# State products beside the next unit's score products, and key transposes one step later

## The chip, the cores and the metric

The kernel runs on one core of one Trainium2 chip. The metric is the device time of one execution in microseconds (us). TensorE is PE, VectorE DVE, ScalarE ACT, GpSimd POOL; SP is the engine whose queue issues the DMAs.

## The reference

A gated linear attention over 4 batches, 8 heads, 768 time steps and a head dimension of 48, then two feed-forward layers over 3072 tokens (384 to 2048 to 384 features):

```python
f = 1.0 / (1.0 + np.exp(-f_logit))
for t in range(S):
    state = f[:, :, t, :, None] * state + np.einsum('bhd,bhe->bhde', k[:, :, t], v[:, :, t])
    y[:, :, t] = np.einsum('bhd,bhde->bhe', q[:, :, t], state)
...
r = np.maximum(x @ w_in, 0.0)
x = (r * r) @ w_out                      # first layer
h = x @ w_in2
x = (h * np.tanh(log1p(exp(h)))) @ w_out2  # second layer
```

## The kernel before

The attention is cut into 24 units: 12 chunks of 64 time steps, each in two halves that hold two batches (y = 0 and 1) and 8 heads. A unit is worked in these pieces, each a small function: the decay (v_min, a_exp, a_ln, v_scan, a_dq, a_dk), q and k times the decay (v_q, v_k), the scores k'q (m_a, PE, tile aq), their causal mask (v_mask), the transposes of k (m_t, PE, tile tr) and their copy to SBUF (a_kn), the output (m_y, PE, tile y) and its copy (a_y), six DMAs that rearrange it (y_dma, ay to ax), its split for the first layer (a_x, v_x), and the product k v that renews the state (m_u, PE, tile uq) with the addition and decay of the state (v_s). The inputs of unit i+2 are loaded by load_f and load_v.

The first layer runs through 96 steps (six blocks of 512 tokens times 16 slices of the hidden dimension). Step j issues do_l1(j), nine matmuls of 128x128 by 128x512 into a PSUM tile h (line 332), and do_l2(j-2), nine more into three accumulators (line 343). Each product is three matmuls, since both factors are split into a high and a low part. Between them ACT and DVE make the activation: act_a(j-1) is a Relu that reads h (line 714), a square and a rounded copy gh; act_b(j-1) is the remainder gl on DVE (line 356). Beside this the weights of the second layer are unpacked (w2_load, w2_abs, w2_bits, w2_split), three steps a slice.

The order is written out by hand. The table START holds the beginning, up to unit 8 and step 18. After it, `put(step, prio, f, ...)` enters a function in a step, and `run` calls a step's functions by rising prio; each engine then works its own instructions in that order. Unit i has s = 4i - 17: m_a in step s behind l1, m_y in step s+2, so that unit i's step s+4 is unit i+1's step s. QUAD = 9: from unit 9 on, aq and uq are computed in four quadrants of 64 by 64, and each takes two PSUM tiles (y = 0, 1).

h, aq, tr, y and uq all come from one PSUM pool with one tag and five buffers; a tile is free when its readers are done:

```python
h_p = ctx.enter_context(tc.tile_pool(name="hps", bufs=5, space=PSUM))
...
a = [h_p.tile([128, 4, C], F32, tag="h", name="aq") for _ in range(2)]
...
u = [h_p.tile([128, 4, D], F32, tag="h", name="uq") for _ in range(2)]
```

Of the kernel before, what the change touches and what calls it, by code (L numbers as in the profile page):

```python
# [22 lines left out]
QUAD = 9  # L23
# [189 lines left out]
def fast_path(ctx: ExitStack, tc: tile.TileContext, flag, qkf, vv, w1, w2, out):  # L213
# [22 lines left out]
    late, done = [], set()  # L236
# [143 lines left out]
    def attention(at, at1):  # L380
# [268 lines left out]
        def put(s, prio, f, *a):  # L649
            todo.setdefault(s, []).append((prio, len(todo.get(s, [])), f, a))  # L650
# [6 lines left out]
        def unit(i, s):  # L657
            put(s - 4, 24, v_min, i)
            put(s - 3, 15, a_exp, i)
            put(s - 3, 31, a_ln, i)  # L660
            put(s - 2, 25, v_scan, i)
            put(s - 2, 32, a_dq, i)
            put(s - 2, 32, a_dk, i)
            put(s - 1, 26, v_q, i, 0)
            put(s - 1, 26, v_q, i, 1)
            put(s - 1, 26, v_k, i)
            put(s - 1, 26, v_end, i)
            put(s + 4 if i >= 8 else 19 + i, 33, v_fmin, i)
            put(s, 110, m_a, i)
            put(s, 111, m_t, i)  # L670
            put(s + 1, 10, v_mask, i, 0)
            put(s + 1, 10, v_mask, i, 1)
            put(s + 1, 14, a_kn, i)
            put(s + 2, 110, m_y, i)
            put(s + 2, 111, m_u, i)
            put(s + 3, 12, a_y, i)
            if i < NE:
                put(s + 3, 112, m_x, i)
            else:
                put(s + 3, 12, y_dma, i)  # L680
            put(s + 3, 22, v_s, i, 0)
            put(s + 3, 22, v_s, i, 1)
            put(s + 4, 16, a_x, i)
            put(s + 4, 30, v_x, i)
            if i < NU - 2:
                put(s + 1, 50, load_f, i + 2)
                put(s + 1, 50, load_v, i + 2)

        for i in range(NU):
            unit(i, (-16, -14, -12, -10, 3, 5, 8, 11)[i] if i < 8 else 4 * i - 17)  # L690
# [252 lines left out]
```

## Time and profile before

| | |
|---|---|
| median of 3 runs | 902.0 us (901.57 to 902.25) |
| profiled execution | 902.64 us, span 900.9 us |
| PE busy | 882.6 us (98%) |
| DVE busy | 676.5 us (75%) |
| ACT busy | 619.0 us (69%) |
| line 332, h (l1 of both layers) | 1728 matmuls, 426.5 us |
| line 343, a (l2 of both layers) | 1146 + 573 matmuls, 388.3 + 223.6 us |

Units 9 to 23 lie between 137 and 430 us of the span, in the second and third of six blocks and what adjoins them. Busy time of PE is modelled, so the chain of waits, which says at each moment what the end waited for, is the better guide; the timelines show each engine's own order, with the idle time before an instruction and what ended it in square brackets.

### The profile page before, as it was taken

What the parts mean: (1) busy time and instruction counts of PE and PEld (TensorE: products, weight loads), DVE (VectorE), ACT (ScalarE), POOL (GpSimd) and SP (SyncE); (2) the same over time, 40 slices, a digit from 0 to 9 for tenths busy, and PEclk for the clock granted to TensorE, in tenths of its full rate; (3) what the DMA queues carried; (4) which work ended last, traced back from release to release, by engine and by line L of the source; (5) the groups of instructions that cost most, each with busy time, mean ns of one, the idle gap of its engine ahead of it and who ended that gap; (6) DMA issues with size and microseconds to landing.
All of it is one profiled execution on the core that took longest, in us unless ns stands there. A gap on an engine that the chain in (4) does not pass through costs nothing.

```text
span 900.9 us, 15172 instructions
## 1 busy us (share of the span) xinstructions
PE 882.6 (98%) x5849; PEld 724.0 (80%) x5849; DVE 676.5 (75%) x1146; ACT 619.0 (69%) x1131; POOL 5.4 (1%) x21
## 2 busy tenths in 40 slices
PE   6899999999999999999999999999999999999997
PEld 6788888888788888778888888888888888888885
DVE  7999976776877878772221788788888788888785
ACT  7798776885887678674544666676666676666664
POOL 2000000000000000000000000000000000000000
PEclk7899999999999999999999999999999999999999
DMA  9972233465536455532453200200200100200001
GB/s 240 349 174 105 68 98 82 156 197 158 189 123 223 135 191 180 186 125 77 169 190 139 71 1 0 71 1 1 71 0 1 71 1 1 71 1 1 36 0 39
DMA packets 34287, 89.93 MB, mean 100 GB/s; under 512 B 5216, under 2 KB 11360, under 8 KB 34208
## 3 DMA queue, kind: packets, MB, share of 16 engines
q1 hardware_dynamic: 34208, 88.89, 30.9%
q8 instruction: 48, 0.79, 0.4%
q14 instruction: 31, 0.25, 0.1%
HBM read 63.70 MB, written 22.02 MB: 95 GB/s over the span
## 4 chain that ended last, share of the span: by engine, by line
PE 96%; DVE 1%; ACT 1%; DMA 1%; issue 1%; SPq 0%; ACTq 0%; DVEq 0%
PE h L332 44%; PE a L343 43%; PE y L524 2%; PE tr L485 1%; PE aq L470 1%; PE at L475 1%; PE y L517 1%; DMA in<-in_qkf_dram 1%; PE u L542 1%; PE uq L537 1%; PE xt L576 0%; ACT kn L507 0%; DVE mv L448 0%; PE a L839 0%; SPq L406 0%
## 5 line engine op out<-in xcount | busy, mean ns | idle before, releaser
L332 PE MATMUL h<-x,w 128*128 128x512 f32 x1728 | 426.5, 391 | 1.2 <-ACT x L601 0.6
L343 PE MATMUL a<-gh,w 128*128 128x512 f32 x1146 | 388.3, 393 | 0.0
L332 PEld LDWEIGHTS h<-x,w 128*128 128x128 f32 x1728 | 324.8, 188 | 70.6 <-DVE x L605 0.9
L343 PEld LDWEIGHTS a<-gh,w 128*128 128x128 f32 x1146 | 215.2, 188 | 46.1
L343 PE MATMUL a<-gl,w 128*128 128x512 f32 x573 | 223.6, 391 | 0.0
L781 ACT ACTIVATE e<-e 128x512 f32<-128x512 f32 x95 | 60.1, 632 | 117.5 <-DVE e L780 117.5
L356 DVE TENSOR_TENSOR gl<-r,gh 128x512 fp32r<-128x512 f32 x96 | 65.8, 686 | 80.3 <-ACT gh L351 79.9
L343 PEld LDWEIGHTS a<-gl,w 128*128 128x128 f32 x573 | 107.7, 188 | 21.7 <-DVE gl L356 0.4
L780 DVE TENSOR_SCALAR e<-h 128x512 f32<-128x512 f32 x95 | 65.7, 692 | 60.8 <-PE h L332 58.2
L714 ACT ACTIVATE r<-h 128x512 f32<-128x512 f32 x96 | 56.7, 591 | 55.0 <-PE h L332 54.5
L775 ACT ACTIVATE r<-u,cst 128x512 f32<-128x512 f32 x94 | 67.9, 723 | 8.7 <-DVE u L789 2.7
L789 DVE SCALAR_TENSOR_TENSOR u<-e 128x512 f32<-128x512 f32 x95 | 65.9, 694 | 10.1 <-ACT e L781 0.7
L356 DVE TENSOR_TENSOR gl<-g,gh 128x512 fp32r<-128x512 f32 x95 | 65.7, 691 | 0.0
L777 DVE TENSOR_TENSOR e<-h,u 128x512 f32<-128x512 f32 x94 | 64.2, 683 | 0.0
L784 DVE TENSOR_TENSOR g<-e,r 128x512 f32<-128x512 f32 x94 | 64.2, 682 | 0.0
L351 ACT ACTIVATE gh<-r 128x512 fp32r<-128x512 f32 x96 | 60.7, 633 | 3.1
L715 ACT ACTIVATE r<-r 128x512 f32<-128x512 f32 x96 | 60.7, 632 | 3.1
L351 ACT ACTIVATE gh<-g 128x512 fp32r<-128x512 f32 x95 | 60.2, 633 | 3.0 <-DVE g L808 0.8
L776 ACT ACTIVATE r<-r 128x512 f32<-128x512 f32 x94 | 59.5, 633 | 3.0
L507 ACT ACTIVATE kn<-tr 64x192 f32<-64x192 f32 x88 | 28.4, 322 | 7.5 <-PE tr L485 6.6
L605 DVE TENSOR_TENSOR x<-ax,x 128x384 fp32r<-128x384 f32 x16 | 8.9, 556 | 32.5 <-ACT x L601 32.5
L433 DVE TENSOR_TENSOR_SCAN es<-es,cap 112x520 f32<-112x520 f32 x24 | 29.6, 1235 | 3.1 <-ACT es L429 3.0
(120 smaller groups left out, 707.2 us busy)
## 6 DMA issues: line engine op xcount, KB each, us to landing
r<-in_w_dram SPq DMA_DIRECT2D x16, 768.0 KB, 11.9
sr<-in_w_dram SPq DMA_DIRECT2D x32, 384.0 KB, 3.7
w2d<-sw SPq DMA_DIRECT2D x32, 384.0 KB, 3.4
w<-w2d SPq DMA_DIRECT2D x32, 384.0 KB, 3.5
in<-in_qkf_dram SPq DMA_DIRECT2D x18, 672.0 KB, 5.7
vs<-in_vv_dram SPq DMA_DIRECT2D x48, 96.0 KB, 5.5
x2d<-ot SPq DMA_DIRECT2D x18, 256.0 KB, 2.1
x<-x2d SPq DMA_DIRECT2D x6, 768.0 KB, 5.2
```

The costliest lines, as they stand in the source:

```text
L332: T.matmul(out=ps, lhsT=w[:, k * 128:(k + 1) * 128], rhs=x[:, s, k], start=(i == 0), stop=(i == 8))
L343: T.matmul(out=acc[m], lhsT=w[:, m * 128:(m + 1) * 128], rhs=gx, start=(fc == 0 and i == 0), stop=(fc == FC - 1 and i == 2))
L351: A.activation(out=gh, in_=g, func=AF.Copy)
L356: V.tensor_tensor(out=gl, in0=g, in1=gh.bitcast(F32), op=ALU.subtract)
L715: A.activation(out=r, in_=r, func=AF.Square)
L775: A.activation(out=r, in_=u, func=AF.Ln, bias=two)
L776: A.activation(out=r, in_=r, func=AF.Exp, scale=-1.0)
L777: V.tensor_tensor(out=e, in0=hp, in1=u, op=ALU.mult)
L780: V.tensor_scalar(out=e2, in0=ps, scalar1=20.0, scalar2=None, op0=ALU.min)
L781: A.activation(out=e2, in_=e2, func=AF.Exp)
L784: V.tensor_tensor(out=g, in0=e, in1=r, op=ALU.mult)
L789: V.scalar_tensor_tensor(out=u2, in0=e2, scalar=2.0, in1=e2, op0=ALU.add, op1=ALU.mult)
```

## The change

For units from QUAD on (`late`), four entries move: the transposes m_t from step s to s+1 and their copy a_kn from s+1 to s+2; the state products m_u from s+2 to s+4 and the state's renewal v_s from s+3 to s+5; the load load_f of unit i+2 from s+1 to s+2. Since s+4 is the next unit's s, m_u(i) comes right behind m_a(i+1). Units 22 and 23 have no m_t, m_u or v_s, so it concerns those of units 9 to 21. All else is the same, line numbers from 670 on are one or more higher.

```diff
             put(s, 110, m_a, i)
-            put(s, 111, m_t, i)
+            late = i >= QUAD
+            put(s + late, 111, m_t, i)
             put(s + 1, 10, v_mask, i, 0)
             put(s + 1, 10, v_mask, i, 1)
-            put(s + 1, 14, a_kn, i)
+            put(s + 1 + late, 14, a_kn, i)
             put(s + 2, 110, m_y, i)
-            put(s + 2, 111, m_u, i)
+            put(s + 4 if late else s + 2, 111, m_u, i)
             put(s + 3, 12, a_y, i)
...
-            put(s + 3, 22, v_s, i, 0)
-            put(s + 3, 22, v_s, i, 1)
+            put(s + 5 if late else s + 3, 22, v_s, i, 0)
+            put(s + 5 if late else s + 3, 22, v_s, i, 1)
             put(s + 4, 16, a_x, i)
             put(s + 4, 30, v_x, i)
             if i < NU - 2:
-                put(s + 1, 50, load_f, i + 2)
+                put(s + 1 + late, 50, load_f, i + 2)
                 put(s + 1, 50, load_v, i + 2)
```

PE around step s of unit 10, the difference (- before, + now): h is l1, aq the scores of unit 10, tr its transposes, uq the state products of unit 9, a the accumulators of l2.

```order
 L332 MATMUL h<-x,w_777 128x512 x9
 L470 MATMUL aq<-mv_154,in_144 64x64 x16
-L485 MATMUL tr<-idn,in_144 128x112 x4
+L537 MATMUL uq<-vs_151,kn_157 48x48 x16
 L343 MATMUL a_1609<-gh,w_716 128x512
 L343 MATMUL a_1609<-gl,w_716 128x512
@@ -542,4 +541,5 @@
 L343 MATMUL a_1611<-gh,w_716 128x512
 L332 MATMUL h<-x,w_826 128x512 x9
+L485 MATMUL tr<-idn,in_144 128x112 x4
 L343 MATMUL a_1609<-gh,w_743 128x512
```

uq stands behind aq now, and tr between l1 and l2 of the next step.

DVE in steps s and s+1 of unit 11 before: x is the split of unit 10, wbit are the w2 bits, mv the masked scores, gl the remainders, sw the w2 split, es the scan.

```order
L605 TENSOR_TENSOR x<-ax,x 128x3x128
L356 TENSOR_TENSOR gl<-r,gh 128x512
L460 TENSOR_TENSOR fmin<-fmin,f 112x8
L254 TENSOR_SCALAR wbit<-wbit 128x768
L257 SCALAR_TENSOR_TENSOR wbit<-sr,wbit 128x384 x2
L260 SCALAR_TENSOR_TENSOR wbit<-sr,wbit 128x384 x2
L494 TENSOR_TENSOR mv_155<-aq,cmask 64x4x64 x4
L356 TENSOR_TENSOR gl<-r,gh 128x512
L306 SCALAR_TENSOR_TENSOR sw<-wbit,sw 128x384 x2
L433 SCALAR_TENSOR_TENSOR es_161<-es_161,cap 112x520
```

And now, from the masks on:

```order
L494 TENSOR_TENSOR mv_155<-aq,cmask 64x4x64 x4
L587 TENSOR_TENSOR vs_150<-uq,vs_152 48x4x48 x2
L588 TENSOR_TENSOR vs_150<-vs_150,f 48x384
L587 TENSOR_TENSOR vs_150<-uq,vs_152 48x4x48 x2
L588 TENSOR_TENSOR vs_150<-vs_150,f 48x384
L356 TENSOR_TENSOR gl<-r,gh 128x512
L306 SCALAR_TENSOR_TENSOR sw<-wbit,sw 128x384 x2
L433 SCALAR_TENSOR_TENSOR es_161<-es_161,cap 112x520
```

v_s of unit 10 (lines 587, 588) stands between the masks of unit 11 and gl; before, it stood ahead of the v_q of unit 11.

SP in steps 32 to 34 (unit 12), the difference: w2d are stores of the w2 split, in is load_f, vs load_v, x2d the eviction of a block, ax the first of six DMAs of y_dma.

```order
 L308 DMA w2d_0_101<-sw 128x768
 L308 DMA w2d_1_102<-sw 128x768
-L406 DMA in_144<-in_qkf_dram 112x1536
-L418 DMA vs_152<-in_vv_dram 64x384 x2
+L418 DMA vs_152<-in_vv_dram 64x384 x2
+L406 DMA in_144<-in_qkf_dram 112x1536
 L366 DMA x2d_92<-ot 128x512 x3
 L564 DMA ax<-ay 48x384
```

load_f is issued behind load_v and so nearer to the stores and to y_dma that follow.

## Rows read from the trace of the kernel before

**Rows 1.** The page, part 4: shares of the chain by engine.

```profile
PE 96%; DVE 1%; ACT 1%; DMA 1%; issue 1%; SPq 0%; ACTq 0%; DVEq 0%
```

**Rows 2.** Chain in order of time, unit 17: start us, us, what.

```profile
293.86 0.62 PE aq L470 x32
294.49 0.53 PE tr L485 x4
...
303.26 1.08 PE y L524 x32
304.34 0.51 PE uq L537 x32
304.84 2.29 PE a L343 x9
...
313.27 0.62 PE aq L470 x32
```

**Rows 3.** Chain, places where tr, aq and y stand alone.

```profile
123.27 0.39 PE tr L485 x4
123.66 2.09 PE h L332 x9
...
410.53 0.62 PE aq L470 x32
411.15 2.27 PE a L343 x9
...
419.54 1.08 PE y L524 x32
420.62 2.27 PE a L343 x9
```

**Rows 4.** Chain, the two idle stretches of PE in units 9 to 23.

```profile
234.29 1.33 issue
...
391.10 0.88 issue
```

**Rows 5.** DVE timeline ahead of the second: start us, us, line, operation, [idle before].

```profile
387.24 0.73 DVE L587 TENSOR_TENSOR vs<-uq,vs 48x192 f32<-48x192 f32 x2
...
389.89 1.39 DVE L448 TENSOR_TENSOR mv<-in,eq 48x512 f32<-48x512 f32 x2
391.20 0.68 DVE L452 TENSOR_TENSOR in<-in,es 112x512 f32<-112x512 f32 x1
```

**Rows 6.** Chain, steps 67 to 72 (units 21 and 22).

```profile
371.47 0.62 PE aq L470 x32
...
374.73 2.05 PE h L332 x9
...
391.98 0.69 PE aq L470 x32
...
394.94 2.04 PE h L332 x9
```

**Rows 7.** ACT timeline, units 14 to 21.

```profile
246.62 0.63 ACT L438 ACTIVATE eq<-es 112x512 f32<-112x512 f32 x1 [1.16 <-DVE es L433]
...
278.44 0.55 ACT L250 ACTIVATE wbit<-sr 128x384 f32<-128x384 f32 x1 [1.79 <-DMA sr<-in_w_dram]
...
314.43 0.52 ACT L601 ACTIVATE x<-ax 128x384 fp32r<-128x384 f32 x1 [3.09 <-DMA ax<-ay]
...
365.38 0.60 ACT L365 ACTIVATE ot<-a 128x512 f32<-128x512 f32 x1 [0.79 <-PE a L343]
...
375.17 0.53 ACT L601 ACTIVATE x<-ax 128x384 fp32r<-128x384 f32 x1 [4.96 <-DMA ax<-ay]
...
376.43 0.58 ACT L714 ACTIVATE r<-h 128x512 f32<-128x512 f32 x1
```

**Rows 8.** DVE timeline, unit 14: masks, remainder, split, scan.

```profile
241.99 1.78 DVE L494 TENSOR_TENSOR mv<-aq,cmask 64x256 f32<-64x256 f32 x4
243.80 0.69 DVE L356 TENSOR_TENSOR gl<-r,gh 128x512 fp32r<-128x512 f32 x1
244.41 1.02 DVE L306 SCALAR_TENSOR_TENSOR sw<-wbit,sw 128x384 fp32r<-128x384 f32 x2
245.35 1.23 DVE L433 TENSOR_TENSOR_SCAN es<-es,cap 112x520 f32<-112x520 f32 x1
```

**Rows 9.** The page, part 6: count, KB each, median us to landing.

```profile
in<-in_qkf_dram SPq DMA_DIRECT2D x18, 672.0 KB, 5.7
```

## The prediction

> **What bounds the kernel now.** I read the chain of waits first. It is TensorE (PE) for 96% of the span [rows 1], so a microsecond counts only if PE gains or loses it. In time order the chain then shows one unit of attention between the big matmuls: four steps, each of nine matmuls of l1 (line 332) and nine of l2 (line 343) at 2.04 us a group, and two small groups, aq + tr in step s and y + uq in step s+2 (s = 4i - 17 for unit i). Unit 17 takes from 293.86 to 313.27, 19.41 us [rows 2]; eight groups of 2.04 are 16.32, so the small work costs 3.09. PE idles only twice in units 9 to 23, 1.33 and 0.88 us, both ahead of aq [rows 4]. What the other engines do is read from their timelines: there the reader is to see who is late although PE does not yet wait.
>
> **The small matmuls on PE.** What the order changes is which group follows which. Behind aq the first big group takes 2.27 instead of 2.04, behind y alone also 2.27; tr takes 0.53 behind aq but 0.39 behind a big group, with 2.09 after it [rows 2, 3]. So aq, y and uq leave a tail of about 0.23, tr of 0.05, and stepping from aq to tr costs 0.14. New rows of a unit:
> - step s: aq 0.62, uq, tail 0.23. No row shows uq behind aq. Behind y it takes 0.51 [rows 2]; that is the upper end. If it saves what tr saves where nothing changes, 0.51 - 0.14 = 0.37, which I take: aq and uq are both laid out as 64x64 tiles in the built program, y as 128x64, tr and the big ones as 128x128.
> - step s+1: tr 0.39 + 0.05, some more in the next group: 0.45.
> - step s+2: y 1.08 + 0.23.
> Together 1.22 + 0.45 + 1.31 = 2.98 against 3.09: 0.11 saved in a unit, 1.4 us in the 13 units. With 0.51 for uq it is a loss of 0.03 in a unit, 0.4 us in all; with 0.32 a gain of 2.1.
> The Trainium skill, TensorEngine Tiling (Array Packing), Key Properties, says that changing the tiling mode drains the engine and changing the tile does not; by it uq behind aq has no drain, which is the value that I took. The trace has no aq followed by uq to confirm it.
>
> **The vector work that moves.** v_s(i) is two pairs of additions and two products on VectorE (DVE), 2.65 us from its start to the start of v_q behind it [rows 5]. It stood in step s+3 right ahead of v_q and v_k of the next unit, and v_k is what aq waits for: it ends at 391.88 and aq starts at 391.98 [rows 4, 5]. Moved two steps on, it no longer stands there; both idle stretches of PE go, 2.2 us. What is late next is dealt with below: v_s now stands behind the masks of the next unit, ahead of act_b and of the scan.
>
> **The new wait.** All these products go through five PSUM buffers (tag h, bufs=5). Before, step s held h, two aq and tr: four, one free. Now it holds h, two aq and two uq: all five. So l1 of step s+1 can only start when one of them has been read. In the built program it is, in 12 of the 13 places (units 10 to 22), l1's own buffer of step s: its matmuls wait for ScalarE's Relu (ACT, line 714) of the step before. (At unit 13 it is the first mask.) Before, that Relu had two steps. From l1's end to the next l1 is now 0.62 + 0.37 + 2.27, about 3.2 us. In the trace the Relu ends more than 3.1 us after l1's end in seven of the thirteen places. Take unit 21: l1 ends at 371.47, the next l1 runs from 374.73, the Relu from 376.43 for 0.58, to 377.01 [rows 6, 7]. PE would wait until 377.1, and take 0.07 to restart (aq 0.69 behind an idle stretch against 0.62 [rows 6, 3]).
> The Relu is late because ACT waits in order, first for the six transfers of y into ax (line 601 idles 3.09 and 4.96 us [rows 7]), then in some units for w2 data. Both hang on a_y, an ACT instruction half a unit earlier, so ACT, the SP queue and DVE form a loop of their own that PE hardly drives; only the slack of two steps kept it off PE.
> The Trainium skill, TensorEngine Tiling, Performance Considerations (PSUM Bottleneck), warns of just this for packed matmuls: reading PSUM out may become the bound. In the trace of before no big matmul of units 9 to 23 waits for a reader [rows 4], so by it alone nothing would be expected; the loop above is this kernel's own mechanism.
>
> **What slows that loop.** In a third of the units (14, 17, 20: those with w2_bits in step s) DVE runs without a gap from the masks over act_b and the w2 split to the scan [rows 8], and ACT's line 438 waits for this scan: 1.16 us idle at 246.62, one of three such rows of 1.13 to 1.16 [rows 7]. v_s now stands in that stretch: 2.65 later each, straight on ACT's loop. In unit 20 an eviction that waits for PE by 0.79 anyway (at 365.38 [rows 7]) takes part of it: 3 x 2.65 - 0.79 = 7.2. In the other units DVE idles there or the scan has slack. Moving a_kn one step on leaves ACT's sum up to the scan as it was: nothing.
> Against it: load_f leaves the place behind the w2 loads. In unit 16 ACT waits 1.79 for the second of them [rows 7], with the 672 KB load of in_qkf (5.7 us to landing [rows 9]) issued behind it; relief 0 to 1.8, with a smaller one in unit 19: I take 1.0. The wait of 4.96 for ax in unit 21 could fall towards 3.09 [rows 7]: 0 to 1.9, I take 0.6. X, the loop's delay at unit 21, is 7.2 - 1.0 - 0.6 = 5.6; its bounds are 0 and 9.
>
> **The sum.** At unit 21 PE waits for the loop, so what it saved earlier is swallowed and the end follows from the loop: l1 starts at 377.1 + X instead of 374.73, plus 0.07: 2.4 + X. From there to l1 of unit 22's next step it was 394.94 - 374.73 = 20.21 [rows 6]; now it is eight groups of 2.04 and 2.98: 19.30, a gain of 0.9. Behind that both kernels do the same big work. So 1.5 + X = 7.1 us. The profiled execution took 902.64 (span 900.9), which gives 909.7; the median of the runs is 902.0, 0.64 lower: **909.1 us**.
>
> **Rivals.**
> - The buffers do not bind (faster). Were the Relu to end within 3.1 us of l1 in all 13 places, PE would gain 1.4 and 2.2: 902.0 - 3.6 = 898.4. This needs ACT's wait for ax to fall from 4.96 to below about 2.5 at unit 21; units 11 and 12, where the Relu follows l1 at once, show that it can be so. Against it: moving uq out leaves PE 0.5 us earlier at the next aq while a_y comes no earlier. Chance 0.10.
> - The wait comes, but the scan does not hold ACT (X near 0): 1.5 us, 903.5. This is so if ACT is idle enough behind line 438, but it runs without a gap up to a_y there. Chance 0.12, counted as within 0.2%.
> - load_f collides with y (slower still). In the new SP order it is issued right ahead of the six transfers of y_dma. If each of nine units' ax lands 1 us later, X grows by up to 5: 914. Chance 0.08.
> - The change of neighbours saves nothing on PE. It moves 1.4 us of time that PE spends waiting anyway, and the forecast by less than 0.5.
>
> **How the numbers follow.** The forecast, slower by about 7 us, has 0.70; the collision 0.08, also slower; same 0.12; faster 0.10. A measurement of this kernel tells about 0.2% (1.8 us) from no change. The range has its low end between the second rival and the forecast's low bounds, 901.5, and its high end at the collision, 914.0; it leaves out the faster case and part of the collision.
>
> **What would show it.** In the new profile PE should have idle stretches ahead of line 332 released by ACT's Relu, in the step behind aq + uq, of 0.5 to 3 us in units 10 to 21, some 10 to 11 us in all; units 15, 16, 19 and 21 hold the most. The two stretches ahead of aq should be gone. uq behind aq should take 0.37, tr 0.39. ACT's line 438 should idle 2.6 us longer for the scan in units 14, 17 and 20. The prediction is wrong if PE stays at 98% busy without waits for ACT, if the waits stand ahead of other tiles (the masks, y), or if the small groups cost more than 3.1 a unit.

## The result and the profile after

The changed kernel takes 913.3 us (median of four runs, 913.09 to 914.43) against 901.8 for the kernel before beside it: a ratio of 1.0134, 95% interval 1.0121 to 1.0146, 11.5 us more. Its profiled execution has a span of 911.4 us.

The page of the kernel after, part 4, shares of the chain of waits by engine, answers to [rows 1]:

```profile
PE 70%; DVE 11%; ACT 7%; SPq 4%; DMA 4%; issue 3%; ACTq 0%; DVEq 0%
```

A chain that was TensorE's to 96% now leaves it for 30% of the span and runs over DVE, ACT and the transfers. What PE waits for, after, between 130 and 420 us (line waited at, releaser, us in total, times, longest):

```profile
PE h L332 <- ACT r L715: 6.9, 7, 1.7
PE tr L485 <- DVE mv L494: 3.7, 3, 1.8
PE h L332 <- DVE mv L494: 1.4, 1, 1.4
```

That is 12.0 us in eleven waits. The two stretches ahead of aq of [rows 4] are not among them. The PE timeline after (start us, us, line, operation, shapes, count, idle time and its releaser) has the new pair of neighbours in unit 11, the wait for the Relu in unit 15, and the wait for the masks in unit 14:

```profile
174.20 2.20 PE L332 MATMUL h<-x,w 128*128 128x512 f32 x9
176.33 0.69 PE L470 MATMUL aq<-mv,in 48*64 48x64 f32 x32
176.85 0.54 PE L537 MATMUL uq<-vs,kn 64*48 64x48 f32 x32
177.32 0.50 PE L343 MATMUL a<-gh,w 128*128 128x512 f32 x1
...
244.29 0.57 PE L485 MATMUL tr<-idn,in 112*128 112x112 f32 x4 [1.80 <-DVE mv L494]
...
262.98 2.34 PE L332 MATMUL h<-x,w 128*128 128x512 f32 x9 [1.23 <-ACT r L715]
```

On DVE, unit 14 after answers to [rows 8]. v_s (lines 587 and 588) stands between the masks and gl, and the scan ends 3.82 us after its old place (250.40 against 246.58), of which 1.3 us is the later start of the masks:

```profile
243.29 1.74 DVE L494 TENSOR_TENSOR mv<-aq,cmask 64x256 f32<-64x256 f32 x4
245.07 0.72 DVE L587 TENSOR_TENSOR vs<-uq,vs 48x192 f32<-48x192 f32 x2
245.83 0.55 DVE L588 TENSOR_TENSOR vs<-vs,f 48x384 f32<-48x384 f32 x1
246.40 0.72 DVE L587 TENSOR_TENSOR vs<-uq,vs 48x192 f32<-48x192 f32 x2
247.15 0.55 DVE L588 TENSOR_TENSOR vs<-vs,f 48x384 f32<-48x384 f32 x1
247.63 0.68 DVE L356 TENSOR_TENSOR gl<-r,gh 128x512 fp32r<-128x512 f32 x1
248.23 1.01 DVE L306 SCALAR_TENSOR_TENSOR sw<-wbit,sw 128x384 fp32r<-128x384 f32 x2
249.17 1.23 DVE L433 TENSOR_TENSOR_SCAN es<-es,cap 112x520 f32<-112x520 f32 x1
```

The loop of ACT can be followed between two fixed points, the Relu of unit 14's step s and that of unit 21's. Before, from 238.70 to 377.01 us, ACT waits for:

```profile
ACT x L601 <- DMA ax<-ay: 18.8, 7, 5.0
ACT wbit L250 <- DMA sr<-in_w_dram: 6.2, 4, 1.8
ACT eq L438 <- DVE es L433: 3.4, 3, 1.2
ACT r L714 <- PE h L332: 1.7, 2, 1.0
ACT ot L365 <- PE a L343: 0.8, 1, 0.8
```

After, from 240.01 to 385.74:

```profile
ACT x L601 <- DMA ax<-ay: 16.7, 7, 3.9
ACT eq L438 <- DVE es L433: 9.8, 5, 3.6
ACT wbit L250 <- DMA sr<-in_w_dram: 5.6, 4, 1.7
ACT r L715 <- PE h L332: 3.7, 5, 1.3
ACT ot L365 <- PE a L343: 1.9, 2, 1.1
ACT sw L305 <- DVE wbit L260: 0.4, 2, 0.2
```

The stretch is 7.4 us longer (145.73 against 138.31): 6.4 more of waits for the scan, 3.1 more of waits for PE (lines 715 and 365), 0.4 for the bits, less 2.1 for ax and 0.6 for the w2 loads. ACT starts it 1.3 us later, so unit 21's Relu is 8.7 us late. That is the prediction's X, there put at 5.6.

### The profile page after: what moved, and what is told of

The parts are those of the page before. It is cut to its first block, busy times and chain, and to the rows that moved or that the text cites. A ratio compares the mean times of both kernels' runs of the same rounds, so it can differ in the third digit from the quotient of the medians.

```text
span 911.4 us, 15197 instructions
## 1 busy us (share of the span) xinstructions
PE 883.1 (97%) x5849; PEld 721.5 (79%) x5849; DVE 674.6 (74%) x1146; ACT 618.9 (68%) x1131; POOL 5.3 (1%) x21
## 4 chain that ended last, share of the span: by engine, by line
PE 70%; DVE 11%; ACT 7%; SPq 4%; DMA 4%; issue 3%; ACTq 0%; DVEq 0%
PE h L332 33%; PE a L343 32%; DMA ax<-ay 2%; DVE mv L494 1%; DMA sr<-in_w_dram 1%; DVE vs L587 1%; DVE es L433 1%; ACT r L715 1%; DVE gl L356 1%; ACT r L716 1%; SPq L567 1%; DVE wbit L257 1%; SPq L565 1%; PE y L517 1%; SPq L568 1%
## 5 line engine op out<-in xcount | busy, mean ns | idle before, releaser
L601 ACT ACTIVATE x<-ax 128x384 fp32r<-128x384 f32 x16 | 8.4, 525 | 36.5 <-DMA ax<-ay 36.5
```

## The experiments

All times are medians with the ratio to the kernel before on the same chip. Beside them stands the stretch of the profiled execution from the first big product of step 19 (unit 9) to that of step 75 (unit 23): 273.4 us before, 284.3 after. It is free of the start, where the profiled executions differ by up to 2 us although the work up to there is the same in all.

| kernel | median us | ratio, 95% interval | stretch, us over before |
|---|---|---|---|
| after | 913.3 | 1.0134 [1.0121, 1.0146] | 10.8 |
| e1_load_only | 901.6 | 1.0003 [0.9989, 1.0017] | -0.2 |
| e8_transposes_only | 905.7 | 1.0050 [1.0030, 1.0070] | 4.2 |
| e2_scan_first | 915.3 | 1.0141 [1.0120, 1.0162] | 13.9 |
| e3_shared_banks | 910.3 | 1.0112 [1.0081, 1.0142] | 9.0 |
| e4_shared_scan | 913.5 | 1.0129 [1.0112, 1.0146] | 12.7 |
| e7_shared_vs_behind_gl | 921.6 | 1.0230 [1.0199, 1.0260] | 21.4 |
| e11_before_vs_place | 909.6 | 1.0088 [1.0075, 1.0101] | 8.5 |
| e6_vs_early | 907.1 | 1.0070 [1.0045, 1.0096] | 4.7 |
| e10_vs_first | 907.9 | 1.0065 [1.0051, 1.0078] | 6.9 |
| e5_shared_vs_early | 904.5 | 1.0036 [1.0024, 1.0048] | 2.8 |
| e9_shared_vs_first | 902.5 | 1.0018 [1.0009, 1.0028] | 3.5 |
| e12_shared_vs_mixed | 904.4 | 1.0021 [1.0002, 1.0039] | 2.7 |

### The prediction's theory: the buffers and the scan

**The load alone** (the kernel before with load_f one step later).

```diff
-                put(s + 1, 50, load_f, i + 2)
+                put(s + 1 + (i >= QUAD), 50, load_f, i + 2)
```

> The kernel before with one part of the change alone: load_f of units 11 to 23 one step later. Theory (full buffers and the scan behind v_s): this part costs nothing, 901 to 903 us, ACT's waits for ax within 3 us of the 33.0 us in all that they are before. Rival (load_f collides with the six transfers of y): the waits for ax grow by 5 us or more and the time by 3 us or more, 905 and above.

Measured 901.6, no difference, and ACT's waits for ax are 34.8 us in 14 places against 33.0 in 14 before. The third rival (load_f collides with y's transfers) does not come; neither does the later load relieve anything that shows in the time.

**The scan first** (after, with a_ln and v_scan ahead of v_s).

```diff
-            put(s - 3, 31, a_ln, i)
-            put(s - 2, 25, v_scan, i)
+            put(s - 3, 20 if i > QUAD else 31, a_ln, i)
+            put(s - 3 if i > QUAD else s - 2, 21 if i > QUAD else 25, v_scan, i)
```

> The changed kernel with the scan of units 10 on (and the logarithm that it needs) one place earlier, ahead of v_s on DVE. Theory: ACT's waits for the scan in units 11, 14, 17 and 20 (3.15, 3.56, 3.45, 1.97 us after the change) fall below 1 us, the Relu of unit 21 ends 6 to 8 us earlier, PE still waits for some Relus, 905 to 909 us. Rival (the wait for Relu alone costs, the scan's place is hidden): within 1 us of 913.3.

A miss: 915.3, no gain. ACT no longer waits for the scan at all, but for the bits (9.8 us at line 305, from DVE's line 260), and PE waits 7.3 us for the masks. The scan was only the first to be late: whatever stands in that part of DVE's order is.

**The buffers** (after, with uq in the free columns of aq's two PSUM tiles, so that step s holds three buffers of five).

```diff
-                a = [h_p.tile([128, 4, C], F32, tag="h", name="aq") for _ in range(2)]
+                p = [h_p.tile([128, 4 * (C + D)], F32, tag="h", name="aq") for _ in range(2)]
+                a = [t[:, 0:4 * C].rearrange("p (a t) -> p a t", a=4) for t in p]
+                U[i]["p"] = [t[:, 4 * C:].rearrange("p (a e) -> p a e", a=4) for t in reversed(p)]
...
-                u = [h_p.tile([128, 4, D], F32, tag="h", name="uq") for _ in range(2)]
+                u = U[i + 1]["p"]
```

> The changed kernel with uq in the free part of the two PSUM tiles that aq takes in the same step, so that step s holds three buffers and not five; the order is the same on every engine. Theory: PE's waits ahead of line 332 for the Relu of the step before (6.9 us) go, and those of tr for the masks too; the slow loop of ACT and DVE is left, hidden by a slack of two steps for the most part: 899 to 904 us. Rival (the loop bounds the time whatever the buffers are): 910 to 913 us, with the waits ahead of other tiles.

A miss that overturns half of the theory: 910.3. PE's waits in e3, 130 to 430 us:

```profile
PE a L343 <- DVE gl L356: 4.7, 5, 1.9
PE a L343 <- ACT ot L365: 1.0, 1, 1.0
PE h L332 <- ACT x L603: 0.4, 1, 0.4
```

Every wait for the Relu and for the masks is gone, and the kernel is still 9.0 us slower in the stretch. The lateness of DVE now reaches PE through another door: the second group of products (line 343) needs gl. In three of the five places (3.7 of the 4.7 us) this gl stands behind v_s, in the other two behind v_x. Two of these waits, of 1.93 and 1.49 us, cost more than their length. In unit 14, in windows of 2 us (window, length, busy us and instructions of PE, PEld, DVE, ACT, POOL, granted clock, DMA share, GB/s):

```profile
244.00:246.00 2.00, 1.74 (x35) 1.20 (x33) 1.91 (x5) 1.94 (x6) 0.00 (x0) 1.00 0.89 330
246.00:248.00 2.00, 0.33 (x1) 0.33 (x2) 1.95 (x5) 0.13 (x1) 0.00 (x0) 0.94 0.02 9
248.00:250.00 2.00, 2.00 (x6) 1.54 (x6) 2.00 (x4) 0.27 (x1) 0.00 (x0) 0.50 0.54 212
250.00:252.00 2.00, 2.00 (x8) 1.59 (x7) 1.87 (x4) 1.97 (x6) 0.00 (x0) 0.70 0.99 304
252.00:254.00 2.00, 2.00 (x11) 1.65 (x10) 0.38 (x1) 1.91 (x6) 0.00 (x0) 1.00 0.72 221
```

Behind y's 32 half-wide products, one big one and 1.93 us of idling, PE's granted clock falls to 0.50 (1.2 of 2.4 GHz) and is back by 252. That step takes 9.16 us; the same step of a unit without a wait takes 5.39 (unit 10 of e3). So the wait of 1.93 costs 3.8.

**Both** (e3 with the scan first, the two diffs above).

> Both edits together: shared PSUM tiles and the scan ahead of v_s. Theory: no wait on PE in units 10 to 22 is left, neither for the Relu nor ahead of aq, and the saving on PE (0.11 us a unit, 1.4 in all) and the two idle stretches (2.2) come out: 898 to 900 us. Rival (the new neighbours on PE save nothing, restarts and tails eat it): 900.5 to 902.

A miss again, 913.5: line 343 waits 9.1 us for gl, line 305 on ACT 9.8 for the bits.

### The theory that took its place: where v_s stands on DVE

Before, v_s ran ahead of v_q and v_k, and soon behind these DVE comes to its wait for v_x' input: it had time there (27.2 us of such waits in 11 places between 130 and 412 us before, 53.1 in 14 places after). Now v_s stands in the stretch that has no idle time on DVE in a third of the units. Three kernels put that to the test.

**The place alone** (the kernel before, with v_s in its new place; a constant is added in place of uq, so that no PSUM tile is held; the state products are made but left out of the state).

```diff
-                    V.tensor_tensor(out=new[:, :, b], in0=u[64 * b:64 * b + 48], in1=old[:, :, b], op=ALU.add)
+                    V.tensor_tensor(out=new[:, :, b], in0=idn[64 * b:64 * b + 48, 0:48].unsqueeze(1).to_broadcast([48, 4, D]),
+                                    in1=old[:, :, b], op=ALU.add)
...
-            put(s + 3, 22, v_s, i, 0)
-            put(s + 3, 22, v_s, i, 1)
+            put(s + 5 if i >= QUAD else s + 3, 22, v_s, i, 0)
+            put(s + 5 if i >= QUAD else s + 3, 22, v_s, i, 1)
```

> The kernel before with v_s alone, from unit 9 on, in the place that the change gives it on VectorE (between the next unit's masks and its act_b), TensorE's order untouched. So that no PSUM is held longer by it, v_s adds a constant in place of the state products (the products are made and left unread): the running state is left out of the outputs of units 11 to 23, the time of VectorE's work is the same. Theory (the place alone makes act_b and the scan late): waits of L343 for act_b as in e3_shared_banks and ScalarE's waits for the scan at about 3.5 us in units 11, 14, 17 and 20: 905 to 911 us. Rival (the place costs nothing without PSUM held): 899 to 902.

909.6: with PE's order as before and no PSUM buffer held longer, v_s' place alone makes the stretch 8.5 us longer. PE's waits in e11, 130 to 430 us, and, last, ACT's for the scan between 237 and 384:

```profile
PE a L343 <- DVE gl L356: 4.6, 5, 1.5
PE a L343 <- ACT ot L365: 0.8, 1, 0.8
PE h L332 <- ACT r L715: 0.5, 1, 0.5
PE h L332 <- ACT x L602: 0.3, 1, 0.3
...
ACT eq L438 <- DVE es L433: 11.2, 4, 3.7
```

The addition takes as long as the real one (0.71 to 0.75 us a pair against 0.72), so what differs is the place, and that v_s has no uq to wait for.

**v_s where DVE waits** (after, with v_s in step s+4, and v_x behind it but for units 11, 15, 19 and 23). In e6 uq has its own buffers, in e5 it shares aq's.

```diff
-            put(s + 5 if late else s + 3, 22, v_s, i, 0)
-            put(s + 5 if late else s + 3, 22, v_s, i, 1)
+            put(s + 4 if late else s + 3, 112 if late else 22, v_s, i, 0)
+            put(s + 4 if late else s + 3, 112 if late else 22, v_s, i, 1)
...
-            put(s + 4, 30, v_x, i)
+            put(s + 4, 113 if late and i % 4 != 3 else 30, v_x, i)
```

> The changed kernel with v_s and v_x moved as in e5_shared_vs_early, but with the state products in two PSUM buffers of their own: only VectorE's order differs from the changed kernel's. Theory now: X, the lateness of ScalarE and VectorE, goes (8.7 us), but the big products of the next step still wait for the Relu, by the lag that the kernel before had there: 901 to 906 us, with some 6 us of waits of L332 on the Relu left in units 15 to 21 and the scan's waits back at about 1.1 us each. The prediction's theory (the five buffers alone set the loss, v_s' place is worth little): 910 to 913.

> The changed kernel with the state products in the free columns of the score products' two PSUM tiles (as in e3_shared_banks), and from unit 9 on v_s one step earlier and behind act_b, and v_x behind it, so that VectorE does v_s in the time in which it waited for v_x's transfer (5.17 us ahead of v_x in unit 14 of e3) and no longer between the masks and act_b of the next step. Theory now (v_s' new place on VectorE makes act_b, the scan and ScalarE late, whatever PSUM holds): the waits of L343 for act_b (4.7 us in e3), the waits of L438 for the scan (19.4 us) and the low clock behind them go, and about 1.5 us of the saved weight loads is left: 898 to 901 us. Rival 1 (the later transposes with a_kn make ScalarE late): nothing gained against e3, 908 to 911. Rival 2 (the wait for a_x' transfer is what makes all late, v_s only shows it): 904 to 908, with the waits of L343 back in units 14, 17 and 20.

e6 takes 907.1: about half of the loss goes (in the stretch 10.8 falls to 4.7), and what is left on PE is one line, between 130 and 430 us:

```profile
PE h L332 <- ACT r L715: 6.9, 5, 2.4
```

These are the waits that the five buffers bring, and their sum stays although the loop of ACT, between its two fixed points, is only 1.9 us longer than before (140.24 against 138.31) and not 7.4. e5, with the buffers shared too, takes 904.5 and 2.8 us in the stretch: better than each cure alone, but 3.5 us above what was expected. The time lies in the second rival's range; its sign does not come, since line 343 waits for no gl, only 1.1 us for an eviction. The timeline of DVE in e5 shows one reason. In units 15 and 21, v_s and v_x and so the masks stood behind a w2 split that waits for ACT (unit 15 here):

```profile
256.06 1.03 DVE L306 SCALAR_TENSOR_TENSOR sw<-wbit,sw 128x384 fp32r<-128x384 f32 x2 [3.72 <-ACT sw L305]
257.12 0.73 DVE L589 TENSOR_TENSOR vs<-aq,vs 48x192 f32<-48x192 f32 x2
...
260.25 1.76 DVE L496 TENSOR_TENSOR mv<-aq,cmask 64x256 f32<-64x256 f32 x4
```

**v_s behind gl** (e3 with v_s in the same step, behind act_b).

```diff
-            put(s + 5 if late else s + 3, 22, v_s, i, 0)
-            put(s + 5 if late else s + 3, 22, v_s, i, 1)
+            put(s + 5 if late else s + 3, 33 if late else 22, v_s, i, 0)
+            put(s + 5 if late else s + 3, 33 if late else 22, v_s, i, 1)
```

> e3_shared_banks with v_s in the same step, but behind act_b instead of ahead of it. Theory now: act_b comes 2.65 us earlier, so the waits of L343 for it go (4.7 us and what the clock lost behind three of them); the scan is as late as in e3, so that ScalarE's waits for it stay at about 3.5 us in units 11, 14, 17 and 20: 903 to 907 us. If act_b's lateness has another cause (the masks or v_x ahead of it): 908 to 911, with the waits of L343 unchanged.

The worst of all, 921.6, and a clear miss. The gl that was to gain is on time: the two longest waits of e3 do not come back. But v_s still stands in the stretch. The scan waits rise from 19.4 us in 11 places in e3 to 29.9 in 13, with 2.7 us each in units 10, 13, 16 and 19, where e3 has at most 0.8. Line 343 now waits for gl in other steps: in four of seven places this gl stands behind v_x and so behind ACT's wait for ax, in three behind the scan. In unit 15 PE waits 3.03 us for one (timeline of e7, two rows of DVE and one of PE):

```profile
265.18 0.56 DVE L607 TENSOR_TENSOR x<-ax,x 128x384 fp32r<-128x384 f32 x1 [4.63 <-ACT x L603]
265.66 0.68 DVE L356 TENSOR_TENSOR gl<-r,gh 128x512 fp32r<-128x512 f32 x1
...
266.40 0.50 PE L343 MATMUL a<-gl,w 128*128 128x512 f32 x1 [3.03 <-DVE gl L356]
```

### What is left without both

**The w2 work behind v_s and v_x** (e6 and e5 with this; v_x behind v_s in all late units).

```diff
-            put(s + 4, 113 if late and i % 4 != 3 else 30, v_x, i)
+            put(s + 4, 113 if late else 30, v_x, i)
...
-                put(23 + 3 * f, 58, w2_abs, f, half)
-                put(25 + 3 * f, (62, 70)[half], w2_split, f, half)
-            put(24 + 3 * f, 60, w2_bits, f)
+                put(23 + 3 * f, 114, w2_abs, f, half)
+                put(25 + 3 * f, (116, 117)[half], w2_split, f, half)
+            put(24 + 3 * f, 115, w2_bits, f)
```

> The same order of VectorE as in e9_shared_vs_first, with the state products in two PSUM buffers of their own again, so that the waits of the big products for the Relu are the only thing of the change's cost that is left. Theory: 5 to 7 us of waits of L332 on the Relu, each with some 0.3 us of restart, less 1.5 us of saved weight loads: 903 to 907 us. If the waits on the Relu fall with VectorE's earlier masks and act_b (ScalarE less late): 900 to 903.

> As e5_shared_vs_early, but act_b, v_s and v_x now stand ahead of the work on W2 in VectorE's order of the step (in e5 v_s and v_x stood behind L306, which waited 3.4 to 3.7 us for ScalarE's L305 in units 15 and 21, and behind the sign bits in unit 20). Theory (v_s' place on VectorE is what is left of the loss once PSUM is shared): the waits of L526 (1.9 us), of L343 for the eviction (1.1) and of L332 for v_x (0.7) go, with what the restarts behind them cost: 899 to 901.5 us. Rival (what is left in e5 is ScalarE's own lateness by the later a_kn): 903 to 906 us, with waits of L343 for L365 or of L332 for the Relu in their place.

e10, with two buffers for uq, takes 907.9, a little more than expected; PE's waits are 5.7 us for the Relu. e9, without the buffers' wait, takes 902.5, a little more than expected too. The two differ in PSUM alone: the buffers' share is 5.4 us by the medians, 3.4 in the stretch. Two other pairs differ in the same way and give less: 3.0 and 1.8 us between the kernel after and e3, 2.6 and 1.9 between e6 and e5. PE's waits in e9:

```profile
PE h L332 <- ACT x L603: 1.8, 2, 0.9
PE h L332 <- DVE x L607: 1.5, 2, 0.8
PE y L526 <- ACT r L717: 0.6, 1, 0.6
```

Most of this, 3.3 us, are waits of the first big products of a block for that block's input, v_x of units 11, 15 and 19, now behind v_s; e5 has 0.7 us of these. The last kernel turned that back.

```diff
-            put(s + 4, 113 if late else 30, v_x, i)
+            put(s + 4, 113 if late and i % 4 != 3 else 30, v_x, i)
```

> As e9_shared_vs_first, but in units 11, 15 and 19 v_x stands ahead of act_b and v_s again, as in e5_shared_vs_early, because the first big products of the next block read it one step later. e9 lost 1.5, 2.0 and 3.2 us in the three steps in which L332 waits for that block's input (waits of 0.73, 0.92 and 1.64 us); e5 lost nothing at the first two and 0.8 at the third. Theory (what is left in e9 is v_x' lateness behind v_s): these waits go in the first two and fall below 0.7 us in the third: 897 to 900.5 us. Rival (ScalarE's a_x is late by its transfer, whatever VectorE does): the waits of L332 for L603 stay, 901 to 903.

904.4, not better. The wait in unit 11 goes, but those for a_x in units 15 and 19 stay (0.54 and 0.78 us), as the rival had it: ACT's a_x there waits for its transfer, whatever DVE does. Its time, 901 to 903, was too low as well. y waits 1.0 us for a Relu, too, so five buffers are tight even with uq in aq's tiles. No version beats the kernel before.

**The transposes alone** (the kernel before with m_t, a_kn and load_f one step later, m_u and v_s in their old places).

```diff
-            put(s, 111, m_t, i)
+            late = i >= QUAD
+            put(s + late, 111, m_t, i)
...
-            put(s + 1, 14, a_kn, i)
+            put(s + 1 + late, 14, a_kn, i)
...
-                put(s + 1, 50, load_f, i + 2)
+                put(s + 1 + late, 50, load_f, i + 2)
```

> The kernel before with only one part of the change: from unit 9 on the transposes, a_kn and load_f one step later, the state products and v_s where they were. The state products then stand one step behind their transposes, and a_kn of the same step is done on ScalarE behind the Relu and the square of the step ahead. Theory: PE waits for a_kn ahead of the state products by the lag of the Relu less about 3 us, nothing in units 9 to 12 and 1 to 4 us in units 13 to 21: 908 to 916 us. Rival (the lag shrinks as soon as PE waits once, so that the later units wait for nothing): 902 to 905.

905.7, between theory and rival: uq does wait for a_kn, but in two units only (13 and 21), 2.8 us in four pieces, because PE's wait lets ACT catch up: behind it, the Relu of unit 14's step s ends 0.63 us after l1, against 4.43 before. The first pair costs far more than its 1.81 us (timeline of PE in e8):

```profile
223.90 1.15 PE L524 MATMUL y<-mv,vs 112*64 112x64 f32 x32
226.46 0.28 PE L537 MATMUL uq<-vs,kn 64*48 64x48 f32 x2 [1.41 <-ACT kn L507]
227.15 1.05 PE L537 MATMUL uq<-vs,kn 64*48 64x48 f32 x30 [0.40 <-ACT kn L507]
```

The step takes 9.92 us against 5.92 before, and the granted clock is 0.50 from 228 to 230 us. In the kernel after, uq stands two steps later and none of PE's waits is for a_kn, so this loss is not a part of the change's 11.5 us.

## Why the prediction was right, and where it was not

The forecast was 7.1 us slower, in a range of 901.5 to 914.0; 11.5 came. That 913.3 lies within the range is in part luck: the high end came from the collision of load_f, which e1 shows not to happen, and the loop's own upper bound, X = 9, gives only 902.0 + 1.5 + 9 = 912.5. By the prediction's own steps:

- **The small matmuls.** Right. aq and uq take 0.52 + 0.47 = 0.99 us from start to start (176.33 to 177.32), as 0.62 + 0.37 had it; aq gives up its 0.10 of tail to a neighbour in the same 64x64 layout. A unit without a wait (unit 10 of e3) takes 19.28 us instead of 19.41: 0.13 saved, predicted 0.11.
- **The stretches ahead of aq.** Right: both are gone.
- **The new wait.** Right in kind and size, not in place. The text had 10 to 11 us ahead of line 332 for the Relu, and named waits for the masks as a sign of error. There are 6.9 us of the one and 5.1 of the other, 3.7 of them ahead of tr in units 11, 14 and 17: tr, too, draws a buffer, one of aq's, and the text asked of l1 alone which buffer it gets.
- **The end follows from the loop.** Right: 1.5 + 8.7 = 10.2, the spans differ by 10.5. So the error lies in X.
- **X, 8.7 instead of 5.6.** This is the term that was mis-sized. The scan in units 14 to 21: 6.4 us more waiting, against 7.2. The relief: 2.1 for ax and 0.6 for w2, 2.7 in all, against 1.6. What the sum did not have at all are 3.1 us of waits of ACT for PE and 1.3 us that the loop is late already at unit 14, after PE's waits in units 10 to 13 and a wait of ACT for the scan of unit 11 that grew from 0.67 to 3.15 us. The step that failed is the sentence that PE hardly drives this loop: once PE waits, its products come late to ACT, and the delay goes round.
- **The restart, 0.07.** Too small. In the stretch, waits of 12.0 less the 2.2 that were there before, less 1.5 saved (0.11 to 0.13 in 13 units), are 8.3 us, and 10.8 came: on the mean 0.2 us more at each of eleven waits, with the granted clock at 1.00 throughout. A part of it can be seen in the row at 262.98: nine products in 2.34 us, where 2.20 is usual (174.20).
- **The rival "the buffers do not bind", 898.4.** Its price was wrong, and with it the picture that the five buffers bring the loss. e3 makes them not bind and takes 910.3. The text saw v_s' place only as a delay of the scan in three units; e11 shows that the place alone, with no buffer held, costs 8.5 us in the stretch: line 343 waits 4.6 us for gl, and ACT 3.6 to 3.7 us each for the scan in units 11, 14, 17 and 20. The buffers' own share is smaller, 1.8 to 5.4 us by the pair of runs and the measure. The two shares are not to be added: while PE waits for the Relu, DVE catches up, and in the kernel after line 343 never waits for gl.
- **The collision of load_f** does not come (e1).

What stays open: why e5, e9 and e12, without either cause, are still 0.2 to 0.4% slower than before and not 0.4% faster, as 2.2 us of idling and 1.5 us of small work would give. Their waits (3.7, 3.9 and 3.6 us) are shown to stand at the input of a block, at y and at an eviction. That this is the loop of transfers, which PE now meets earlier, is argued, not shown; the later a_kn, which stays in all three, has no run of its own beside these cures. The waits listed would leave them level with the kernel before. In e5 the steps of units 9 to 22 together take 6.9 us more than its steps without a wait would, of which 3.7 are these waits; the rest stands in the same steps or right behind them. In e9's profiled execution (904.5, above its median of 902.5) a stretch of low clock, from 357 to 360 us, adds some 1.7 of its 3.5 us (an estimate: half of the time at 0.50).

## What to carry to other kernels

A piece of work that moves to fill a gap on one engine moves on every engine that works on its result; look there for the stretch without idle time, and price the move by all that stands behind it in that stretch, not by the one wait that shows today. A shared pool of buffers is only one of the doors by which such lateness comes to the engine that bounds, and to close it moves the wait to the next; the test is to undo the move on the second engine alone. Where the engines feed each other in a loop, a delay of one is not a term but goes round: count what the waiting engine's own products do to the others.

## What the runs showed of the hardware

A wait of 1.93 us behind narrow products (y in e3) and waits of 1.41 and 0.40 us around them (y and uq in e8) were followed by a granted clock of 0.50, and cost about twice their length: 3.8 and 4.0 us. A wait of 1.80 us in the kernel after, behind nine full products (the row at 244.29), was not. Yet the width of the work ahead does not tell the two apart. In e10 PE waits 2.02 us ahead of line 332 in unit 14, behind nine full products, until 240.41, and the clock falls. In e6 it waits 2.37 us at the same point of unit 21, until 378.67, and the clock stays. Two windows of e10, then two of e6:

```profile
240.00:242.00 2.00, 1.59 (x5) 1.34 (x6) 1.97 (x5) 1.94 (x4) 0.00 (x0) 0.79 0.15 45
242.00:244.00 2.00, 2.00 (x7) 1.43 (x7) 1.92 (x5) 1.76 (x4) 0.00 (x0) 0.50 0.30 31
...
378.00:380.00 2.00, 1.33 (x6) 1.10 (x7) 1.92 (x5) 1.94 (x5) 0.00 (x0) 1.00 0.69 268
380.00:382.00 2.00, 2.00 (x13) 1.65 (x12) 1.91 (x6) 1.97 (x5) 0.00 (x0) 1.00 0.99 321
```

Even two waits of 0.87 and 0.77 us close together (e9, until 355.28 and 356.55) were followed by 0.50. So a wait of about two microseconds can cost twice its length or little more than its length, and these runs do not show what decides. Between 130 and 430 us the low clock comes in the profiled executions of e2, e3, e4, e7, e8, e9 and e10, and in none of the kernel before, the kernel after, e1, e5, e6, e11 and e12; the first seven carry it in their column of the stretch. The Trainium skill, TensorE: Matmul & The Clock Gate, Part 1 (The HAM clock gate), describes a gate with these two levels that follows how busy the engine has been; the rows agree with the levels.
